# A list scheduler's margins for TensorE behind landings, and preparation ranked by the step that needs it

## The chip, the cores and the metric

The kernel runs on one core of a Trainium2 chip. The metric is the device time of one execution in microseconds; before the change it is 750.58 us, the median of three runs (747.56 to 751.36).

## The reference

Inputs are q, k, v of 4 batches x 8 heads x 768 positions x 64, a projection 64 x 6, and the weights of a gated network. Cut to what matters:

```
q_bucket = sum(bits(q @ proj) * 2**j);  k_bucket = the same of k
mask     = q_bucket[:, :, :, None] == k_bucket[:, :, None, :]
scores   = where(mask, q @ k.T / 8, -1e9)
attn     = softmax(scores);  x = (attn @ v), heads side by side: 4 x 768 x 512
h  = relu(x @ w_in)                       # 512 -> 1024
u, w = h[..., :512], h[..., 512:]
w_n = (w - mean) / sqrt(var + 1e-6)
w_s = einsum('ts,bsd->btd', w_spatial, w_n) + b_spatial[None, :, None]
out = (u * w_s) @ w_out                   # 512 -> 512
```

## The kernel before, in words

**Attention.** The 32 heads are taken as 16 pairs p; head n = 2p + e. A pair has 6 steps i, one for each 128 rows, so there are 96 steps g = 6p + i, written p_i below. A step makes, for both heads, 128 x 768 scores (`scores`, 16 matmuls of 384 columns, tiles `sp`): three products of split float16 halves (`hl`) and a last one of the hash bits (`hk`), which puts masked scores far down. Then for each head VectorE finds the row's bound and copies the scores out (`ex`, L480), ScalarE takes the exponential (`ex`, L483) and its float16 half (`pp`, L487), VectorE or GpSimd ("VG") the rest (`pp`, L491), and a transposing DMA from SyncE's queue turns both (`pt`, L495). TensorE multiplies the turned tiles by v (`weighted`, 18 matmuls, `pv`, L601) some steps later. Heads 2, 4 and 6 work by keys, without turning, and need row maxima first (`row_max`, `mx`).

**Preparation of a pair.** Its q and k are loaded (`load_qk`, 768 KB, one buffer `qk`), hashed (`hash_rows`: 4 matmuls `hp`, two VectorE operations `sg`, 8 small DMAs into `hk`, from GpSimd's queue except for pair 0), and split (`split_qk`: one ScalarE and two VectorE operations, `hl`); v is loaded and split (`load_v`, `split_v`).

**The network.** When 4 pairs (a batch) are done, that batch's network is cut into units of TensorE work (`group`: pieces of 3 matmuls; `vps`, `ups`, `sps`, `ops` by stage), which fill TensorE between the attention steps of the next batch. The last batch's network runs after the last step.

**Weights.** `weights` makes 36 jobs: a load from SyncE's queue (`raw`, four buffers in turn), for 24 of them five more operations (one on ScalarE, four on VectorE, `w`) that make float32 of float64, then two on ScalarE and one on GpSimd that split into halves.

**The planner.** Nothing of this order is written by hand. Every operation is an `Op` with engine, planned duration, predecessors and buffers; `timetable` is a list scheduler: it takes the engine that can start first and, of the operations ready within 0.2 us, the one with the lowest key. The key is `rank` when that is a pair (step, minor), and otherwise (current step, rank), the current step being that of the last planned scores; rank over 8 (the network's units) adds 4 steps. A DMA adds its time to one modelled queue, and its successors get ready when it lands. The operations are then issued in the order of planned starts, so the plan sets only the order of each engine's instructions; on the chip each engine runs them strictly in that order and waits where an operand is not there.

Of the kernel before, what the change touches and what calls it, by code (L numbers as in the profile page):

```python
# [8 lines left out]
F16 = mybir.dt.float16  # L9
# [5 lines left out]
ALU = mybir.AluOpType  # L15
# [3 lines left out]
P = 128  # L19
# [16 lines left out]
def lsh_attention_spatial_gating(  # L36
# [14 lines left out]
    NT = S // P  # L51
    HS = S // 2
# [64 lines left out]
    def timetable(free, banks):  # L117
# [24 lines left out]
        while open_:  # L142
# [95 lines left out]
    def weights():  # L238
# [3 lines left out]
        TINY = 2.0 ** -15 * 1.125  # L242
        RB = 4
        raws = buf("u", UB).new()
# [9 lines left out]
        for i, (src, dst, m, f, key) in enumerate(jobs):  # L254
            c = {}

            def fetch(src=src, m=m, i=i, c=c):
                if i % RB < 2:
                    t = wk.tile([P, NF, HS], F16, tag=f"g{i % RB}", name=f"raw{i}").rearrange("p a q -> p (a q)")
                else:  # L260
                    if i == 2:
                        st["raws"] = wk.tile([P, 2, S], F32, tag="u", bufs=UB, name="raws")
                    t = st["raws"][:, i % RB - 2].bitcast(F16)
# [4 lines left out]
            raw = buf(f"raw{i % RB}", 1).new()  # L268
            hold_ = [raw] if i % RB < 2 else [raw, raws]
            t = op("S", 0.6, fetch, on=hold_, dma=0.95 if src.dtype != F32 else 0.75, rank=R_W)  # L270
# [46 lines left out]
    def load_v(p, *after):  # L317
# [10 lines left out]
        at["v", p] = op("S", 0.5, go, *after, on=[h], rank=R_QK, dma=1.45)  # L328

    def hash_rows(p, *after):  # L330
        qk, k = held["qk", p], (buf("hk", 2) if p != 1 else buf("hk1", 1)).new()
        held["hk", p] = k
        g0, g1 = buf("sg0", 1).new(), buf("sg1", 2).new()
        hp, sg = [], []

        def go():
            hp.append(bank_m(f"hp{p}"))
            for j in range(4):
                nc.tensor.matmul(
                    hp[0][32 * j:32 * j + 32, :HS], lhsT=pj,  # L340
                    rhs=st["qk", p][:, 1 - j // 2, (j % 2) * HS:(j % 2 + 1) * HS],
                    start=True, stop=True, tile_position=(0, 32 * j))

        def bits():
            sg.append(wk.tile([P, HS], F16, tag="sg0", name=f"sg0_{p}"))
            nc.vector.tensor_scalar(sg[0], hp[0][:, :HS], 0.0, hv[:, 0:1], op0=ALU.is_gt, op1=ALU.subtract)

        def scale():
            sg.append(wk.tile([P, HS], F16, tag="sg1", bufs=2, name=f"sg1_{p}"))
            nc.vector.tensor_scalar(sg[1], sg[0], hv[:, 1:2], None, op0=ALU.mult)  # L350
# [3 lines left out]
        t = op("V", 0.3, scale, t, on=[g0, g1], rank=2)  # L354
        at["hk", p] = []
        for j in range(4):
            for e in range(2):
                q, eng = HQ_FIRST[e] if p == 0 else HQ_REST

                def move(j=j, e=e, eng=eng):  # L360
                    eng.dma_start(  # L361
                        out=hkt(p)[D * e:D * e + 2 * NB, 1 - j // 2, (j % 2) * HS:(j % 2 + 1) * HS],
                        in_=sg[1][32 * j + 16 * e:32 * j + 16 * e + 2 * NB, :])
                at["hk", p].append(op(q, 0.53 if q == "G" else 0.75, move, t, on=[g1, k], rank=3, land=2.8 if q == "G" else 1.8))

    def split_qk(p, *after):
# [11 lines left out]
        at["hl", p] = [t] + [  # L378
            op("V", 0.9, lambda to=to, part=part, frm=frm: nc.vector.scalar_tensor_tensor(  # L379
                out=st["hl", p][:, to], in0=st["qk", p][:, part], scalar=SQ, in1=st["hl", p][:, frm],  # L380
                op0=ALU.mult, op1=ALU.subtract), t, on=[qk, h], rank=4)
            for to, part, frm in ((0, 1, 2), (3, 0, 1))]

    def split_v(p, *after):
# [15 lines left out]

        t = op("A", 0.15 + 0.6 * z, high, at["v", p], *after, on=[held["v", p], h], rank=4)
        at["vp", p] = op("V", 0.1 + 0.8 * z, low, t, on=[held["v", p], h], rank=4)

# [65 lines left out]
    def by_queries(p, i, e, g, t, sc):  # L469
# [30 lines left out]
        t = op("A", 0.77, half, t, on=[hx, hp], rank=(g, 1 + e))  # L500
        t = t3 = op("VG", (0.97, 1.68), rest, t, on=[hx, hp], rank=(g, 1 + e))
        at["pt", n, i] = op("S", 1.48, turn, t, on=[hp, ht], rank=(g, 1 + e), dma=TURN)

    def by_keys(p, i, e, g, t, sc):
# [22 lines left out]
        if not wide_:  # L527
            t = op("A", 0.75, half, t, on=[hx, ht], rank=(g, 1 + e))
            t = t3 = op("VG", (0.97, 1.68), rest, t, on=[hx, ht], rank=(g, 1 + e))
        at["pt", n, i] = t  # L530
# [530 lines left out]
```

## Time and the profile before

| | |
|---|---|
| median of the runs | 750.58 us |
| profiled execution, its own time | 750.24 us |
| its span, first to last instruction | 748.4 us |
| TensorE (PE) busy | 631.0 us, 84% |
| VectorE (DVE) busy | 558.5 us, 75% |
| ScalarE (ACT), GpSimd (POOL) busy | 463.5 us, 419.0 us |
| mean granted TensorE clock | 0.945 |
| turning of one `pt`, from issue to landing | 4.1 us, median of 174 |

The times of a profile come from the one profiled execution. PE is a matmul, PEld a weight load. A wait is the idle time of an engine just before an instruction, named by what ended it.

### The profile page before, as it was taken

Reading aid. Unit: us, or ns where it says so; the run is one execution under the profiler, and the core shown is the slowest. Engines: PE = TensorE matmul, PEld = TensorE weight load, DVE = VectorE, ACT = ScalarE, POOL = GpSimd, SP = SyncE. Lnnn points to the kernel's source line nnn. Section 1 sums busy time; section 2 is a strip of 40 time slices with the busy share of each in tenths; the row PEclk is TensorE's granted clock in tenths of the full one; section 3 lists DMA queues with packets and bytes.
Section 4 is the critical chain, followed back from the end, with each engine's and each line's share of the span. In section 5 each row is a group of like instructions: output and inputs, shape, how many; then the busy total and the mean of one; then the engine's idle time right before and its main releaser. Section 6 shows DMA issues by size and latency. Waiting matters only on the chain.

```text
span 748.4 us, 16873 instructions
## 1 busy us (share of the span) xinstructions
PE 631.0 (84%) x6667; PEld 370.7 (50%) x6667; DVE 558.5 (75%) x1009; ACT 463.5 (62%) x707; POOL 419.0 (56%) x451
## 2 busy tenths in 40 slices
PE   3877988967887678789898888879889979989997
PEld 1444755744454445445544545545545445445553
DVE  6889789896999987676879897877677785081250
ACT  3767667787878566656577677566767674332212
POOL 5655554788677669573857565774776552033100
PEclk9788799889998899899999999989999999999999
DMA  5898595799997699899779999897969866001102
GB/s 177 149 201 180 120 218 114 154 223 197 218 222 148 124 188 180 150 187 185 164 166 173 195 149 172 176 174 165 208 122 168 151 117 117 1 1 43 43 1 84
DMA packets 318259, 110.84 MB, mean 148 GB/s; under 512 B 305124, under 2 KB 308196, under 8 KB 318180
## 3 DMA queue, kind: packets, MB, share of 16 engines
q1 hardware_dynamic: 314244, 108.62, 73.9%
q0 software_dynamic: 3840, 1.12, 0.8%
q8 instruction: 52, 0.85, 0.5%
q14 instruction: 27, 0.22, 0.1%
q10 hardware_dynamic: 96, 0.04, 0.0%
HBM read 27.94 MB, written 6.29 MB: 46 GB/s over the span
## 4 chain that ended last, share of the span: by engine, by line
PE 27%; DVE 21%; DMA 13%; issue 10%; ACT 6%; POOL 6%; DVEq 0%; SPq 0%; ACTq 0%; POOLq 0%
DMA pt<-pp 12%; PE sps L696 6%; DVE ex L480 6%; PE ops L696 6%; PE sp L453 4%; DVE pp L491 4%; PE pv L601 4%; ACT pp L487 3%; ACT ex L483 2%; PE ups L696 2%; POOL pp L491 2%; DVE hl L379 2%; PE vpp L696 2%; DVE vr L828 1%; PE vps L696 1%
## 5 line engine op out<-in xcount | busy, mean ns | idle before, releaser
L483 ACT ACTIVATE ex<-ex,nb 128x768 f32<-128x768 f32 x174 | 158.0, 934 | 120.8 <-DVE ex L480 120.5
L601 PE MATMUL pv<-vp,pt 128*128 128x65 f16 (+1 forms) x3132 | 128.3, 198 | 63.7 <-DMA pt<-pp 49.5
L480 DVE TENSOR_SCALAR_CACHE_REDUCE ex<-sp 128x768 f32<-128x768 f32 x174 | 160.0, 949 | 24.9 <-PE sp L453 24.8
L491 POOL TENSOR_TENSOR pp<-ex,pp 128x768 f16<-128x768 f32 x71 | 125.2, 1765 | 88.6 <-ACT pp L487 82.2
L491 DVE TENSOR_TENSOR pp<-ex,pp 128x768 f16<-128x768 f32 x103 | 126.4, 1231 | 57.7 <-ACT pp L487 56.7
L601 PEld LDWEIGHTS <-pt 128*128 128x128 f16 x3132 | 113.7, 100 | 110.3 <-DMA pt<-pp 68.2
L487 ACT CAST pp<-ex 128x768 f16<-128x768 f32 x174 | 138.4, 822 | 0.6
L453 PE MATMUL sp<-hl 64*128 64x384 f16 x1080 | 118.7, 345 | 16.9 <-DVE ex L480 15.6
L696 PE MATMUL sps<-ws,vn 128*128 128x384 f16 x576 | 100.6, 328 | 0.0
L453 PEld LDWEIGHTS <-hl 64*128 64x128 f16 x1104 | 54.0, 98 | 72.3 <-issue 46.1
L361 POOL DMA_DIRECT2D hk<-sg x112 | 59.5, 537 | 43.1 <-PE ups L696 16.0
L696 PEld LDWEIGHTS <-vn 128*128 128x128 f16 x576 | 54.7, 98 | 34.6 <-issue 0.8
L696 PE MATMUL ops<-wo,g 128*128 128x512 f16 x288 | 67.1, 386 | 1.9 <-DVE u L859 1.9
L696 PE MATMUL ups<-xt,wi 128*128 128x384 f16 x348 | 64.2, 333 | 4.3 <-ACT u L864 3.0
L696 PE MATMUL vps<-wi,xt 128*128 128x512 f16 x234 | 56.9, 382 | 2.7 <-ACT vr L779 2.7
L897 POOL TENSOR_TENSOR sy<-sy,u 128x384 f32<-128x384 f32 x24 | 29.3, 1219 | 49.4 <-DVE sy L885 46.4
L633 POOL TENSOR_TENSOR x<-x,xf 128x384 f32<-128x384 f32 x31 | 39.3, 1267 | 26.7 <-DVE x L630 25.9
L453 PE MATMUL sp<-hk 63*128 63x384 f16 (+1 forms) x360 | 51.5, 345 | 2.7 <-DMA hk<-sg 2.7
L696 PEld LDWEIGHTS <-wi 128*128 128x128 f16 x384 | 36.3, 99 | 29.0 <-issue 8.4
L885 DVE SCALAR_TENSOR_TENSOR sy<-sps,bt 128x384 f32<-128x384 f32 x32 | 17.7, 554 | 40.2 <-PE sps L696 40.2
L696 PEld LDWEIGHTS <-g 128*128 128x128 f16 x288 | 27.5, 99 | 33.8 <-issue 4.6
L893 ACT CAST g<-sy 128x384 f16<-128x384 f32 x32 | 16.3, 510 | 42.7 <-POOL sy L897 22.2
(111 smaller groups left out, 855.0 us busy)
## 6 DMA issues: line engine op xcount, KB each, us to landing
qk<-kq SPq DMA_DIRECT2D x16, 768.0 KB, 5.8
out<-o SPq DMA_DIRECT2D x24, 256.0 KB, 4.2
v<-v SPq DMA_DIRECT2D x13, 384.0 KB, 4.7
pt<-pp SPq DMA_TRANSPOSE x174, 4.1
raw<-w_in SPq DMA_DIRECT2D x8, 256.0 KB, 3.5
raws<-w_in SPq DMA_DIRECT2D x8, 256.0 KB
hk<-sg POOLq DMA_DIRECT2D x112, 9.0 KB, 3.5
vf<-v SPq DMA_DIRECT2D x3, 384.0 KB
```

The lines of the kernel that those rows point to most:

```text
L361: eng.dma_start(out=hkt(p)[D * e:D * e + 2 * NB, 1 - j // 2, (j % 2) * HS:(j % 2 + 1) * HS], in_=sg[1][32 * j + 16 * e:32 * j + 16 * e + 2 ...
L453: nc.tensor.matmul(ps[e][:, c - halves[0]], lhsT=src[r, l, rows], rhs=src[r, m, cs], start=(a == 0), stop=(a == len(passes) - 1))
L480: nc.vector.tensor_scalar(ex, st["sc", p, i][e], -ISQ, None, op0=ALU.mult, op1=ALU.min, accum_out=st["nb", n][:, i:i + 1])
L483: nc.scalar.activation(st["e32", n, i], st["e32", n, i], AF.Exp, bias=st["nb", n][:, i:i + 1], scale=-1.0)
L487: nc.scalar.copy(st["pp", n, i][:, 0], st["e32", n, i])
L491: eng.tensor_tensor(out=st["pp", n, i][:, 1], in0=st.pop(("e32", n, i)), in1=st["pp", n, i][:, 0], op=ALU.subtract)
L601: nc.tensor.matmul(o, lhsT=l, rhs=m, start=(i == 0 and k == 0), stop=(i == NT - 1 and k == len(todo_) - 1))
L633: eng.tensor_add(st["x", n], st["x", n], st["f"])
L696: nc.tensor.matmul(c[0], lhsT=l(), rhs=r(), start=(j == 0), stop=(j == len(products) - 1))
L885: nc.vector.scalar_tensor_tensor(out=y[0], in0=c[0], scalar=1.0 / (SN * SW), in1=bt[:, hs], op0=ALU.mult, op1=ALU.add)
L893: nc.scalar.copy(gt[h][0][:, d], y[0])
L897: t1 = op(*POST[last], lambda: either(t1).tensor_mul(y[0], y[0], u[h][:, d]), t, done["u", d, h], on=[hy, hu[h]], rank=2)
```

## The change

Four things are altered, all of them in what the planner is told; the arithmetic stays, and each engine has the same work apart from 5 of the 174 `pp` rests, which move from VectorE to GpSimd.

- When an operation ends, those of its successors that run on TensorE and are not scores are taken as ready later than before: 0.5 us (`LATE`) after an operation of another engine, 2.5 us (`LATE_D`) after a DMA.
- Preparation has a step of its own as rank: hashing and splitting of pair p stand at step 6p - 3 (6p - 8 for pairs with a head by keys), splitting of v at 6p - 1. Before, they counted as of the current step.
- The `pp` rest has planned durations of 1.1 us on VectorE and 1.75 us on GpSimd, before 0.97 and 1.68.
- The weights' loads may be planned 10 us earlier (`W_FROM` 20, before 30). `RB` becomes a list, with the same values i % 4.

```diff
             for a in o.then:
-                a.ready = max(a.ready, come + (0.0 if a.e == o.e and not o.land and not o.dma else X))
+                late = (LATE_D if o.dma else LATE) if a.e == "P" and not (isinstance(a.rank, tuple) and a.rank[1] == 0) else 0.0
+                a.ready = max(a.ready, come + (0.0 if a.e == o.e and not o.land and not o.dma else X + late))
...
-        RB = 4
+        RB = [i % 4 if i < MANY else i % 2 for i in range(36)]
...
+    def urgent(p):
+        return NT * p - (8 if keys(p) else 3)
...
-        t = op("P", 0.8, go, at["qk", p], *after, on=[qk], rank=3, need=("m", 1))
-        t = op("V", 0.62, bits, t, on=[g0], rank=2, gives="m")
+        t = op("P", 0.8, go, at["qk", p], *after, on=[qk], rank=(urgent(p), 3), need=("m", 1))
+        t = op("V", 0.62, bits, t, on=[g0], rank=(urgent(p), 2), gives="m")
...
-        t = op("A", 1.42, high, at["qk", p], *after, on=[qk, h], rank=4)
+        t = op("A", 1.42, high, at["qk", p], *after, on=[qk, h], rank=(urgent(p), 4))
...
-        t = op("A", 0.15 + 0.6 * z, high, at["v", p], *after, on=[held["v", p], h], rank=4)
+        t = op("A", 0.15 + 0.6 * z, high, at["v", p], *after, on=[held["v", p], h], rank=(NT * p - 1, 4))
...
-        t = t3 = op("VG", (0.97, 1.68), rest, t, on=[hx, hp], rank=(g, 1 + e))
+        t = t3 = op("VG", (1.1, 1.75), rest, t, on=[hx, hp], rank=(g, 1 + e))
...
+    LATE, LATE_D = 0.5, 2.5
+    MANY = 36
-    W_FROM, W_EVERY = 30.0, 3.6
+    W_FROM, W_EVERY = 20.0, 3.6
```

In the rows below a name ends in the buffer's running number, the lines after the change stand six further down, and only the first row of each run of matmuls is shown. The first place is TensorE between the scores of steps 9_2 and 9_3 (`sp9_2`, `sp9_3`), before:

```order
L453 MATMUL sp9_2_0_5259<-hl9_4508 128x384
...
L601 MATMUL pv18_5285<-vp1_89,pt18_0_5187 128x65
...
L601 MATMUL pv19_5309<-vp1_89,pt19_0_5218 128x65
...
L696 MATMUL sps0_3_1_5328<-ws0_75,vn0_0_3301 128x384
...
L601 MATMUL pv18_5285<-vp1_89,pt18_1_5307 128x65
...
L453 MATMUL sp9_3_0_5381<-hl9_4508 128x384
```

The same place on TensorE after the change, where `vps1_1` is a unit of the next batch's network:

```order
L459 MATMUL sp9_2_0_5283<-hl9_4462 128x384
...
L607 MATMUL pv18_5304<-vp1_89,pt18_0_5192 128x65
...
L702 MATMUL vps1_0_5022<-wi0_101,xt7_4888 128x512
...
L607 MATMUL pv19_5334<-vp1_89,pt19_0_5221 128x65
...
L702 MATMUL vps1_1_5356<-wi0_101,xt4_3127 128x512
...
L459 MATMUL sp9_3_0_5384<-hl9_4462 128x384
...
L607 MATMUL pv18_5304<-vp1_89,pt18_1_5324 128x65
```

The products of `pt18_1` stood ahead of the scores of 9_3 and stand behind them now; 15 matmuls of 384 columns ahead of them have become 15 of 512 columns.

The second place is the first step of pair 6. On SyncE's queue its q and k (`qk6`) stood, before, ahead of the turning of `pt8_2`:

```order
L265 DMA raws_480<-w_sp 128x384 x2
L313 DMA qk6_2331<-kq 128x1536
L647 DMA_TRANSPOSE xt3_2376<-xs3_2260 128x12x128
L495 DMA_TRANSPOSE pt8_2_2407<-pp8_2_2303 128x12x128
L495 DMA_TRANSPOSE pt9_2_2419<-pp9_2_2306 128x12x128
```

After the change the load stands behind the turning of `pt11_2`, two weight loads just ahead of it:

```order
L501 DMA_TRANSPOSE pt10_2_2882<-pp10_2_2835 128x12x128
L501 DMA_TRANSPOSE pt11_2_2901<-pp11_2_2876 128x12x128
L267 DMA raws_238<-w_out 128x256 x2
L315 DMA qk6_2969<-kq 128x1536
L328 DMA v32_6_2974<-v 128x768
```

It has moved back past 14 turnings, those of seven steps, and with it the hashing of pair 6 on TensorE: `hp6` stood right behind the scores of 5_0 and now stands behind those of 5_5, in the last gap ahead of 6_0, after the change so:

```order
L459 MATMUL sp5_5_0_3102<-hl5_2086 128x384
...
L702 MATMUL ups0_0_0_3095<-xt1_1498,wi0_101 128x384
...
L345 MATMUL hp6_3157<-qk6_2969,hc_73 32x384 x4
L437 MATMUL mp6_3168<-vc6_3139,ones_72 128x128
L607 MATMUL pv10_2919<-vp1_89,pt10_3_3020 128x65
...
L702 MATMUL ups0_3_0_3281<-xt0_1013,wi0_101 128x384
...
L607 MATMUL pv11_2979<-vp1_89,pt11_4_3209 128x65
...
L459 MATMUL sp6_0_0_3370<-hl6_3100 128x384
```

Between `hp6` and the scores stand 42 matmuls of the network, four sets of 18 value products and `mp6`.

The third place is VectorE at the start, where `sg` are the hash bits and `hl` the split of q and k of pair 0, before:

```order
L346 TENSOR_SCALAR sg0_0_121<-hp0_114,hc_73 128x384
L350 TENSOR_SCALAR sg1_0_126<-sg0_0_121,hc_73 128x384
L379 SCALAR_TENSOR_TENSOR hl0_119<-qk0_108,hl0_119 128x768 x2
L398 SCALAR_TENSOR_TENSOR vp0_88<-v32_0_110,vp0_88 128x12x64
L346 TENSOR_SCALAR sg0_1_153<-hp1_144,hc_73 128x384
```

The same place after the change:

```order
L385 SCALAR_TENSOR_TENSOR hl0_114<-qk0_108,hl0_114 128x768 x2
L352 TENSOR_SCALAR sg0_0_129<-hp0_121,hc_73 128x384
L356 TENSOR_SCALAR sg1_0_133<-sg0_0_129,hc_73 128x384
L404 SCALAR_TENSOR_TENSOR vp0_88<-v32_0_110,vp0_88 128x12x64
L352 TENSOR_SCALAR sg0_1_152<-hp1_146,hc_73 128x384
```

The two splits have moved ahead of the hash bits, and so ahead of the DMAs that write `hk`.

More of the change, by code (lines that the diff above doesn't have):

```diff
@@ L257, in fetch @@
             def fetch(src=src, m=m, i=i, c=c):
-                if i % RB < 2:
-                    t = wk.tile([P, NF, HS], F16, tag=f"g{i % RB}", name=f"raw{i}").rearrange("p a q -> p (a q)")
+                if RB[i] < 2:
+                    t = wk.tile([P, NF, HS], F16, tag=f"g{RB[i]}", name=f"raw{i}").rearrange("p a q -> p (a q)")
                 else:
@@ L262, in fetch @@
                         st["raws"] = wk.tile([P, 2, S], F32, tag="u", bufs=UB, name="raws")
-                    t = st["raws"][:, i % RB - 2].bitcast(F16)
+                    t = st["raws"][:, RB[i] - 2].bitcast(F16)
                 c["raw"] = t[:, :m * (4 if src.dtype != F32 else 2)].bitcast(src.dtype)
@@ L267, in weights @@
             z = m / 256
-            raw = buf(f"raw{i % RB}", 1).new()
-            hold_ = [raw] if i % RB < 2 else [raw, raws]
+            raw = buf(f"raw{RB[i]}", 1).new()
+            hold_ = [raw] if RB[i] < 2 else [raw, raws]
             t = op("S", 0.6, fetch, on=hold_, dma=0.95 if src.dtype != F32 else 0.75, rank=R_W)
@@ L363, in move @@
                         in_=sg[1][32 * j + 16 * e:32 * j + 16 * e + 2 * NB, :])
-                at["hk", p].append(op(q, 0.53 if q == "G" else 0.75, move, t, on=[g1, k], rank=3, land=2.8 if q == "G" else 1.8))
+                at["hk", p].append(op(q, 0.53 if q == "G" else 0.75, move, t, on=[g1, k], rank=(urgent(p), 3), land=2.8 if q == "G" else 1.8))
     def split_qk(p, *after):
@@ L380, in split_qk @@
                 out=st["hl", p][:, to], in0=st["qk", p][:, part], scalar=SQ, in1=st["hl", p][:, frm],
-                op0=ALU.mult, op1=ALU.subtract), t, on=[qk, h], rank=4)
+                op0=ALU.mult, op1=ALU.subtract), t, on=[qk, h], rank=(urgent(p), 4))
             for to, part, frm in ((0, 1, 2), (3, 0, 1))]
@@ L399, in low @@
                                            in1=part(x)[:, :, :, D:2 * D], op0=ALU.mult, op1=ALU.subtract)
[L401 to L402 removed]
+        t = op("A", 0.15 + 0.6 * z, high, at["v", p], *after, on=[held["v", p], h], rank=(NT * p - 1, 4))
+        at["vp", p] = op("V", 0.1 + 0.8 * z, low, t, on=[held["v", p], h], rank=(NT * p - 1, 4))
     def mean_v(p, *after):
@@ L528, in by_keys @@
             t = op("A", 0.75, half, t, on=[hx, ht], rank=(g, 1 + e))
-            t = t3 = op("VG", (0.97, 1.68), rest, t, on=[hx, ht], rank=(g, 1 + e))
+            t = t3 = op("VG", (1.1, 1.75), rest, t, on=[hx, ht], rank=(g, 1 + e))
         at["pt", n, i] = t
```

2 lines of the change are left out of this document (1 added, 1 removed).

## The prediction

> **What bounds the kernel now.** I read the page first, for the span and for the chain of work that ended last.
>
> ```profile
> span 748.4 us, 16873 instructions
> PE 631.0 (84%) x6667; PEld 370.7 (50%) x6667; DVE 558.5 (75%) x1009; ACT 463.5 (62%) x707; POOL 419.0 (56%) x451
> ...
> PE 27%; DVE 21%; DMA 13%; issue 10%; ACT 6%; POOL 6%; DVEq 0%; SPq 0%; ACTq 0%; POOLq 0%
> DMA pt<-pp 12%; PE sps L696 6%; DVE ex L480 6%; PE ops L696 6%; PE sp L453 4%; DVE pp L491 4%; PE pv L601 4%; ACT pp L487 3%; ACT ex L483 2%; PE ups L696 2%; POOL pp L491 2%; DVE hl L379 2%; PE vpp L696 2%; DVE vr L828 1%; PE vps L696 1%
> ```
>
> PE is the fullest engine but no engine is full, and the largest single entry of the chain is not computing: it is the turning of `pt`, 12%. An average over stages hides which wait ends last, so the second view is the table by stretches: start, pairs 0 to 3, pairs 4 to 7, pairs 8 to 15, and the end without attention.
>
> ```profile
> core 0: us, PE busy (x) PEld busy (x) DVE busy (x) ACT busy (x) POOL busy (x), PEclk, DMA share, GB/s
> 0.00:12.00 12.00, 3.83 (x20) 1.07 (x22) 8.05 (x12) 3.78 (x4) 6.46 (x17) 1.00 0.50 169
> 12.00:147.00 135.00, 111.49 (x1182) 75.27 (x1179) 117.84 (x235) 91.27 (x144) 79.28 (x94) 0.86 0.79 161
> 147.00:300.00 153.00, 118.33 (x1448) 70.97 (x1449) 135.72 (x239) 115.32 (x183) 114.11 (x115) 0.92 0.96 189
> 300.00:620.00 320.00, 276.89 (x3282) 157.51 (x3281) 250.10 (x436) 213.43 (x304) 198.29 (x204) 0.97 0.89 165
> 620.00:748.40 128.40, 120.44 (x744) 65.85 (x742) 46.77 (x90) 39.69 (x74) 20.91 (x22) 1.00 0.15 41
> ```
>
> Until 300 us DVE is 87 to 89% full (117.84 of 135, 135.72 of 153). From 300 to 620 us it is 78% and PE 87%: PE is idle for 43.1 us there. The third view, PE's waits in that stretch, says for whom:
>
> ```profile
> PE pv L601 <- DMA pt<-pp: 34.3, 29, 2.5
> PE pv L601 <- DVE x L630: 7.5, 4, 2.3
> PE sp L453 <- DVE ex L480: 1.1, 2, 0.5
> ```
>
> These three are the whole 43 us. The scores wait 1.1 us for VectorE, so VectorE does not set the pace in this stretch; PE does, with its stops at value products whose `pt` has not landed. Between 147 and 300 us it is mixed:
>
> ```profile
> PE pv L601 <- DMA pt<-pp: 9.5, 7, 1.9
> PE sp L453 <- DVE ex L480: 9.3, 9, 1.8
> PE pv L601 <- DVE x L630: 6.3, 3, 5.2
> ```
>
> What such a stop does stands in the timeline of PE around step 9_3, the first place of the order:
>
> ```profile
> 362.75 1.15 PE L453 MATMUL sp<-hl 64*128 64x384 f16 x12
> 363.74 0.49 PE L453 MATMUL sp<-hk 63*128 63x384 f16 x4
> 364.23 1.26 PE L601 MATMUL pv<-vp,pt 128*128 128x65 f16 x36
> 365.33 2.60 PE L696 MATMUL sps<-ws,vn 128*128 128x384 f16 x15
> 370.23 0.72 PE L601 MATMUL pv<-vp,pt 128*128 128x65 f16 x18 [2.30 <-DMA pt<-pp]
> 370.88 1.84 PE L453 MATMUL sp<-hl 64*128 64x384 f16 x12
> ```
>
> PE stops for 2.30 us, and the scores of 9_3, which do not need that tile, stand behind the stop; everything that hangs on them starts later.
>
> **The change part by part.** First the margin of 2.5 us. To see what it buys I counted PE's work between a step's scores and its value products in both orders, with durations of this trace:
>
> ```profile
> 344.97 1.41 PE sp L453 x16
> ...
> 347.34 2.92 PE sps L696 x18
> ...
> 352.32 1.20 PE pv L601 x36
> 353.52 1.29 PE vps L696 x6
> ```
>
> At the first place, between `sp9_2` and the products of `pt18_1`, there were 36 value products and 15 matmuls of 384 columns, 1.20 + 15 x 2.92 / 18 = 3.6 us. Now there are 36 value products, 15 matmuls of 512 columns and a set of scores, 1.20 + 15 x 1.29 / 6 + 1.41 = 5.8 us. The difference, 2.2 us, covers the stop of 2.30 us but for 0.1. Over all tiles of pairs 8 to 15 the same count from a tile's own scores to its value products rises from 9.3 to 11.5 us for the first head of a pair and from 11.5 to 13.1 for the second; for pairs 4 to 7 from 9.8 to 11.8 and from 11.7 to 13.6. The stops have a mean of 34.3 / 29 = 1.2 us and a longest of 2.5. So from 300 us on I take four fifths of them away: -27.4 us, with bounds of 0 and -34.3. Between 147 and 300 us VectorE is full and the tiles come later; I take half of 9.5: -4.7, bounds 0 and -9.5.
>
> Second, the clock. Where PE has stood, it runs at half the granted clock next:
>
> ```profile
> 364.00:371.20 7.20, 4.90 (x77) 3.36 (x75) 6.21 (x11) 4.97 (x8) 7.18 (x8) 1.00 0.78 169
> 371.20:374.60 3.40, 3.40 (x36) 1.92 (x31) 2.09 (x5) 1.22 (x3) 3.24 (x4) 0.50 0.79 150
> ```
>
> The same row by row: 1.00 with the stop in it, 0.50 in the 3.4 us behind it. By the table the clock costs (1 - 0.97) x 277 = 8.3 us of PE's time from 300 to 620 us and (1 - 0.92) x 118 = 9.5 from 147 to 300. A third of the 17.8 us goes with the stops: -6, bounds 0 and -14. The Trainium skill speaks against this term: its page TensorE: Matmul & The Clock Gate, in the table of "Why this matters for your kernels", names idle gaps of more than some 3 us as what halves the clock. By that rule stops of at most 2.5 us cost no clock, and the sum would be 6 us higher. The rows do not bear it out: a stop of 2.30 us was enough here, so I keep the term.
>
> Third, the start (third place of the order). The timeline of VectorE before:
>
> ```profile
> 7.43 0.62 DVE L346 TENSOR_SCALAR sg<-hp,hc 128x384 f16<-128x384 f32 x1 [1.37 <-PE hp L339]
> 8.09 0.36 DVE L350 TENSOR_SCALAR sg<-sg,hc 128x384 f16<-128x384 f16 x1
> 8.36 2.07 DVE L379 SCALAR_TENSOR_TENSOR hl<-qk,hl 128x768 f16<-128x768 f32 x2
> ```
>
> The first scores wait for the `hk` landings, which the hash bits set off:
>
> ```profile
> 16.29 0.51 PE L453 MATMUL sp<-hk 63*128 63x384 f16 x2 [2.68 <-DMA hk<-sg]
> ```
>
> With the two splits ahead, the bits end 2.07 us later, less some 0.2 that the splits start earlier: +1.9, between 1 and 3; nothing covers it, since PE has only this to do. The weights' first operations on ScalarE and VectorE, now right ahead and behind of step 0_0's `ex`, lie in waits there. For the rest of the weights' work, the same on each engine and only earlier, I take 0, between -4 and +4: VectorE is 87% full in that stretch whichever way it is dealt.
>
> Fourth, pair 6 (second place). Its load stands seven steps later on SyncE's queue, behind two weight loads that must wait for their buffers, and `hp6` stands in the last gap ahead of 6_0. Durations:
>
> ```profile
> L480 DVE TENSOR_SCALAR_CACHE_REDUCE ex<-sp 128x768 f32<-128x768 f32 x174 | 160.0, 949 | 24.9 <-PE sp L453 24.8
> L483 ACT ACTIVATE ex<-ex,nb 128x768 f32<-128x768 f32 x174 | 158.0, 934 | 120.8 <-DVE ex L480 120.5
> L487 ACT CAST pp<-ex 128x768 f16<-128x768 f32 x174 | 138.4, 822 | 0.6
> L491 POOL TENSOR_TENSOR pp<-ex,pp 128x768 f16<-128x768 f32 x71 | 125.2, 1765 | 88.6 <-ACT pp L487 82.2
> L361 POOL DMA_DIRECT2D hk<-sg x112 | 59.5, 537 | 43.1 <-PE ups L696 16.0
> ...
> qk<-kq SPq DMA_DIRECT2D x16, 768.0 KB, 5.8
> ...
> hk<-sg POOLq DMA_DIRECT2D x112, 9.0 KB, 3.5
> ```
>
> GpSimd takes up the eight `hk` issues behind the `pp` of `pt10_5`, so from the end of the scores of 5_5: two VectorE and one ScalarE exponential step with its half, 2 x 0.95 + 0.93 + 0.82, the rest on GpSimd 1.77, eight issues 8 x 0.54, landing 3.5, together 13.2 us. PE has in that gap 9 + 42 network matmuls (51 x 0.162 = 8.3), four sets of 18 value products (2.4), the hash and a small product (about 1.3): 12.0 us. The scores would stop for 1.2 us, and longer if the load (5.8 us) holds VectorE at `hl6`. I take +3, between 0 and 10. Much work in the gap is drawn from later gaps, not lost.
>
> Fifth, what is late next. With some 30 us less in the way from 300 us on, the same VectorE work falls into less time, 250.1 us in some 290 instead of 320, 86%, near the fill of the stretch before. There the scores waited 9.3 us in 153, which would be 19 in 320; now it is 1.1. I take +8 in between, bounds 0 and 20. The 5 rests that move to GpSimd (1.77 against some 1.23 us each) change little of this, 0. The waits for `x`, 13.8 us, stay: `pv` has two banks and the distance from a pair's last products to the next pair's first stays at about 4 us of PE work in the order.
>
> Sixth, the end: the second unit of `sps2` now stands ahead of the last value products and fills part of the 8 idle us behind 620: -1, between -4 and 0.
>
> Sum: -27.4 - 4.7 - 6 + 1.9 + 0 + 3 + 8 - 1 = -26.2 us. The span of 748.4 becomes 722.2; the profiled execution took 750.24, 1.8 more than its span, so 724.0. The median of the runs lies 0.3 above the profiled one; I say 724.
>
> **The rivals.** *VectorE takes over.* Until 300 us it is 87 to 89% full and the scores wait for it; if the queues behind it behave so at 86% too, 20 us are given back instead of 8, the half of the stops before 300 us is nothing, and the clock gives 3 instead of 6: -26.2 + 12 + 4.7 + 3 = -6.5, 744. For it speaks the first half of the kernel; against it that 250.1 us at 89% would fit into 281 us, so VectorE alone allows 39 us less. The Trainium skill's page Perfetto Trace Analysis, Identifying the Most-Contended Engine, leans to it: matmul busy time is said to be no measure of how near TensorE is to its limit, and occupancy is for the others; by that the 87% of PE count for little and VectorE's 78% for more. The rows agree only until 300 us.
>
> *Preparation comes too late, and the time rises.* If PE does not set the pace from 300 us on, but the chain of scores, `ex`, `pp` and turning does (73% of the chain is not PE), the stops only move, and the hole at pair 6 stays: the load late by its 5.8 us and the split and hash behind it hold the scores of 6_0 by 10 us, and the start costs 1.9: 750.2 + 12 = 762. It decides as soon as the hole costs more than the stops give. Against it: 1.1 us of waiting for `ex`, and in all other pairs from 1 on 16 us of PE work or more still stand between hash and first scores.
>
> *More than I say.* All stops go (-43.8), the clock gives 12, nothing is late next and pair 6 fits: -43.8 - 12 + 1.9 - 1 = -55, 695. Against it: never so far was PE more than 94% full, and 277 of 320 us would become all but full.
>
> That nothing moves is excluded by the order.
>
> **How the numbers follow.** My forecast, with its own range of 710 to 738 us, has 0.56; VectorE taking over 0.18, half of it on each side of the line below; too late 0.15; more than I say 0.11. A measurement can tell about 0.5% of 750.6 us, so faster means under 746.8 and slower over 754.3. Faster: 0.56 + 0.09 + 0.11 = 0.76; the same 0.09; slower 0.15. For 8 in 10 I leave out most of the slower rival (0.13) and the far part of the faster one (0.07): 704 to 750 us.
>
> **What would show it.** Right: PE's waits for `pt` from 300 us to the last scores fall to under 10 us, with the scores of a step ahead of the late products; the granted clock rises over 0.945; scores wait for `ex` between 5 and 12 us there; the last scores end some 25 us sooner; the first scores' `hk` part starts near 18.2 us; a stop of 1 to 10 us at 6_0. Wrong: the stops stay, or turn one for one into waits for `ex`, `x` or `hk`; VectorE stands at `hl6` for over 10 us; the stretch behind the last scores grows.

## The result, and the profile after

The median of four runs after the change is 719.4 us (717.81 to 722.25), of four runs of the kernel before 749.57 us (747.56 to 751.36). The ratio is 0.960, 95% interval 0.956 to 0.9645. Ratios, here and below, leave out single runs that the record marks as slow (one of margin_pv and a few of the kernel before); medians are of all runs. The profiled execution took 722.25 us, its span 720.5, against 750.24 and 748.4 before. The forecast was 724.0.

The head of the page, and the chain of work that ended last:

```profile
span 720.5 us, 16877 instructions
PE 632.9 (88%) x6667; PEld 371.5 (52%) x6667; DVE 550.1 (76%) x1004; ACT 463.1 (64%) x707; POOL 427.0 (59%) x456
...
PE 35%; DVE 28%; DMA 13%; ACT 11%; issue 9%; POOL 2%; SPq 0%; DVEq 0%; ACTq 0%; POOLq 0%
DMA pt<-pp 10%; DVE ex L486 9%; PE sps L702 8%; PE sp L459 7%; PE ops L702 6%; PE pv L607 6%; DVE pp L497 5%; ACT pp L493 4%; ACT ex L489 3%; DVE hl L385 3%; PE ups L702 3%; PE vpp L702 2%; PE mx L459 2%; DVE vr L834 1%; DVE bs L791 1%
```

PE does the same work in nearly the same busy time (632.9 us, before 631.0). Span less busy time is its idle time: 748.4 - 631.0 = 117.4 us before, 720.5 - 632.9 = 87.6 after. So the change took 29.8 us of idle time from PE and added 1.9 us of busy time, 27.9 together. In the chain PE and VectorE have come forward (27 to 35%, 21 to 28%).

The stretches of the prediction were cut at round times. To set like against like they are cut here at the first scores of pair 4, the first scores of pair 8 and the last scores of each kernel; first before, then after (the columns are the prediction's):

```profile
12.00:146.90 134.90, 111.39 (x1181) 75.19 (x1177) 117.74 (x235) 91.17 (x144) 79.28 (x94) 0.86 0.79 161
146.90:310.60 163.70, 126.52 (x1540) 76.15 (x1539) 140.67 (x247) 120.85 (x191) 118.03 (x120) 0.92 0.96 188
310.60:620.00 309.40, 268.80 (x3194) 152.42 (x3192) 245.25 (x429) 208.00 (x296) 194.36 (x198) 0.97 0.89 165
620.00:748.40 128.40, 120.44 (x744) 65.85 (x742) 46.77 (x90) 39.69 (x74) 20.91 (x22) 1.00 0.15 41
```

```profile
12.00:149.10 137.10, 116.94 (x1197) 76.55 (x1195) 112.61 (x235) 95.27 (x154) 81.25 (x94) 0.85 0.79 164
149.10:301.10 152.00, 123.15 (x1493) 73.08 (x1492) 137.57 (x243) 115.42 (x179) 113.36 (x119) 0.93 1.00 188
301.10:598.40 297.30, 275.05 (x3243) 157.74 (x3242) 245.54 (x426) 210.96 (x302) 204.38 (x206) 0.96 0.95 176
598.40:720.50 122.10, 114.57 (x728) 63.20 (x726) 45.75 (x90) 37.92 (x71) 21.11 (x23) 1.00 0.17 43
```

In pairs 8 to 15 PE's idle time falls from 309.4 - 268.8 = 40.6 to 297.3 - 275.05 = 22.2 us. The stretch is 12.1 us shorter only, because 6.3 us more of PE's work stand in it; the stretch behind the last scores has 5.9 us less work and is 6.3 us shorter. In pairs 4 to 7 idle time falls from 37.2 to 28.8, in pairs 0 to 3 from 23.5 to 20.2. VectorE's share in pairs 8 to 15 rises from 79 to 83%.

PE's waits from the first scores of pair 8 to the last scores (total, times, longest), before and after:

```profile
PE pv L601 <- DMA pt<-pp: 31.8, 28, 2.3
PE pv L601 <- DVE x L630: 7.5, 4, 2.3
PE sp L453 <- DVE ex L480: 1.1, 2, 0.5
```

```profile
PE pv L607 <- DVE x L636: 6.5, 3, 5.4
PE pv L607 <- DMA pt<-pp: 5.0, 9, 1.0
PE sp L459 <- DVE ex L486: 4.7, 7, 2.4
PE sps L702 <- ACT vr L785: 2.0, 1, 2.0
PE mp L437 <- POOL xf L625: 2.0, 1, 2.0
```

The stops for `pt` are all but gone. Of the 26.8 us, 3.6 came back as waits of the scores for `ex`, and some 5.5 as single waits that were not there before, the last two rows and three shorter ones. The place of the prediction's first order rows, step 9_2 to 9_3, in PE's timeline after the change:

```profile
351.58 1.15 PE L459 MATMUL sp<-hl 64*128 64x384 f16 x12
352.57 0.49 PE L459 MATMUL sp<-hk 63*128 63x384 f16 x4
352.99 0.72 PE L607 MATMUL pv<-vp,pt 128*128 128x65 f16 x18
353.55 0.81 PE L702 MATMUL vps<-wi,xt 128*128 128x512 f16 x3
354.19 0.71 PE L607 MATMUL pv<-vp,pt 128*128 128x65 f16 x18
354.74 2.75 PE L702 MATMUL vps<-wi,xt 128*128 128x512 f16 x12
357.43 1.15 PE L459 MATMUL sp<-hl 64*128 64x384 f16 x12
358.41 0.49 PE L459 MATMUL sp<-hk 63*128 63x384 f16 x4
358.94 0.72 PE L607 MATMUL pv<-vp,pt 128*128 128x65 f16 x18
```

No row ends in a wait. The products that stopped PE for 2.30 us now stand behind the scores of 9_3, and their tile is there.

### The profile page after: what moved, and what is told of

Its sections match the earlier page's. It is cut to its first block, busy times and chain, and to the rows that moved or that the text cites. A ratio compares the mean times of both kernels' runs of the same rounds, so it can differ in the third digit from the quotient of the medians.

```text
span 720.5 us, 16877 instructions
## 1 busy us (share of the span) xinstructions
PE 632.9 (88%) x6667; PEld 371.5 (52%) x6667; DVE 550.1 (76%) x1004; ACT 463.1 (64%) x707; POOL 427.0 (59%) x456
## 4 chain that ended last, share of the span: by engine, by line
PE 35%; DVE 28%; DMA 13%; ACT 11%; issue 9%; POOL 2%; SPq 0%; DVEq 0%; ACTq 0%; POOLq 0%
DMA pt<-pp 10%; DVE ex L486 9%; PE sps L702 8%; PE sp L459 7%; PE ops L702 6%; PE pv L607 6%; DVE pp L497 5%; ACT pp L493 4%; ACT ex L489 3%; DVE hl L385 3%; PE ups L702 3%; PE vpp L702 2%; PE mx L459 2%; DVE vr L834 1%; DVE bs L791 1%
## 5 line engine op out<-in xcount | busy, mean ns | idle before, releaser
L497 POOL TENSOR_TENSOR pp<-ex,pp 128x768 f16<-128x768 f32 x76 | 136.1, 1792 | 93.2 <-ACT pp L493 85.5
L486 DVE TENSOR_SCALAR_CACHE_REDUCE ex<-sp 128x768 f32<-128x768 f32 x174 | 160.0, 949 | 22.0 <-PE sp L459 21.9
L497 DVE TENSOR_TENSOR pp<-ex,pp 128x768 f16<-128x768 f32 x98 | 123.8, 1266 | 44.8 <-ACT pp L493 43.3
L607 PEld LDWEIGHTS <-pt 128*128 128x128 f16 x3132 | 116.5, 100 | 61.4 <-issue 34.3
L459 PE MATMUL sp<-hl 64*128 64x384 f16 x1080 | 124.5, 351 | 25.4 <-DVE ex L486 23.8
L459 PEld LDWEIGHTS <-hl 64*128 64x128 f16 x1104 | 56.8, 100 | 88.6 <-issue 64.2
L702 PE MATMUL ups<-xt,wi 128*128 128x384 f16 x348 | 66.2, 334 | 2.9 <-DVE sg L352 2.8
L367 POOL DMA_DIRECT2D hk<-sg x112 | 59.5, 537 | 14.7 <-PE pv L607 6.8
L459 PE MATMUL sp<-hk 63*128 63x384 f16 (+1 forms) x360 | 54.7, 348 | 8.4 <-DMA hk<-sg 5.9
L903 POOL TENSOR_TENSOR sy<-sy,u 128x384 f32<-128x384 f32 x24 | 27.2, 1134 | 49.3 <-DVE sy L891 48.9
L891 DVE SCALAR_TENSOR_TENSOR sy<-sps,bt 128x384 f32<-128x384 f32 x32 | 17.7, 552 | 36.2 <-PE sps L702 36.1
L639 POOL TENSOR_TENSOR x<-x,xf 128x384 f32<-128x384 f32 x31 | 34.6, 1115 | 11.1 <-DVE x L636 8.7
L702 PEld LDWEIGHTS <-xt 128*128 128x128 f16 x288 | 25.9, 97 | 29.1 <-issue 3.7
```

The source lines that it names most:

```text
L367: eng.dma_start(out=hkt(p)[D * e:D * e + 2 * NB, 1 - j // 2, (j % 2) * HS:(j % 2 + 1) * HS], in_=sg[1][32 * j + 16 * e:32 * j + 16 * e + 2 ...
L459: nc.tensor.matmul(ps[e][:, c - halves[0]], lhsT=src[r, l, rows], rhs=src[r, m, cs], start=(a == 0), stop=(a == len(passes) - 1))
L486: nc.vector.tensor_scalar(ex, st["sc", p, i][e], -ISQ, None, op0=ALU.mult, op1=ALU.min, accum_out=st["nb", n][:, i:i + 1])
L497: eng.tensor_tensor(out=st["pp", n, i][:, 1], in0=st.pop(("e32", n, i)), in1=st["pp", n, i][:, 0], op=ALU.subtract)
L607: nc.tensor.matmul(o, lhsT=l, rhs=m, start=(i == 0 and k == 0), stop=(i == NT - 1 and k == len(todo_) - 1))
L639: eng.tensor_add(st["x", n], st["x", n], st["f"])
```

## The experiments

The theory: PE runs its instructions strictly in order, so a value product planned for the moment of its tile's landing stops everything behind it whenever the landing is late; the margin puts other work ahead, and that is the gain. Rival one: the other edits (preparation by its step, weights earlier, the durations of the rests) make the gain. Rival two: it is luck, since any edit of the planner deals the order anew. All kernels compute the whole reference. In the table "idle" is PE's (span less busy time of the profiled execution), "8 to 15" the idle time between the first scores of pair 8 and the last scores, "pt" PE's waits for the turned tiles in the whole span, all in us. Busy, idle and pt are of one profiled execution each, which lies between 7.9 us under the kernel's median (late_d1) and 4.9 us over it (after_x016); PE's work is the same in all. The runs were made on several chips, and each ratio is to the kernel before beside it, whose medians were 748.0 to 750.5 us; so differences of medians below are good to some 2 us.

| kernel | median | ratio to before (95%) | PE busy | idle | 8 to 15 | pt |
|---|---|---|---|---|---|---|
| before | 749.57 | 1 | 631.0 | 117.4 | 40.6 | 49.5 |
| after | 719.40 | 0.960 (0.956 to 0.9645) | 632.9 | 87.6 | 22.2 | 5.7 |
| no_margin | 742.89 | 0.991 (0.987 to 0.995) | 635.2 | 110.8 | 41.0 | 54.7 |
| margin_only | 734.05 | 0.977 (0.971 to 0.984) | 634.5 | 96.0 | 25.9 | 8.5 |
| x016 | 739.97 | 0.986 (0.980 to 0.9915) | 627.3 | 109.1 | 32.9 | 56.7 |
| late_d1 | 730.49 | 0.973 (0.967 to 0.979) | 619.7 | 101.2 | 32.1 | 24.5 |
| margin_late | 731.82 | 0.976 (0.9675 to 0.985) | 631.6 | 99.2 | 25.6 | 17.7 |
| margin_pv | 719.11 | 0.958 (0.943 to 0.974) | 623.6 | 93.6 | 21.1 | 10.4 |
| ranks_only | 755.03 | 1.010 (1.006 to 1.013) | 639.3 | 117.0 | 41.3 | 58.2 |
| qk_first | 734.68 | 0.981 (0.9725 to 0.989) | 634.5 | 97.9 | 22.4 | 10.4 |
| pv_only | 729.84 | 0.973 (0.969 to 0.978) | 625.8 | 99.3 | 24.8 | 7.3 |
| after_x016 | 724.76 | 0.9685 (0.9625 to 0.9745) | 633.6 | 94.2 | 27.6 | 10.3 |
| pv_x016 | 724.33 | 0.968 (0.963 to 0.974) | 632.0 | 86.7 | 29.8 | 14.5 |
| landing_only | 733.32 | 0.980 (0.973 to 0.987) | 633.7 | 98.7 | 21.9 | 13.8 |

### The margin alone, everything but the margin, half of it, and an edit that means nothing

**margin_only** is the kernel before with the margins and nothing else of the change:

```diff
+                late = (LATE_D if o.dma else LATE) if a.e == "P" and not (isinstance(a.rank, tuple) and a.rank[1] == 0) else 0.0
-                ... X))
+                ... X + late))
+    LATE, LATE_D = 0.5, 2.5
```

> The kernel before with the margins of 0.5 and 2.5 us alone; ranks, planned durations of the rest and the weights' start are as before. In its order TensorE has 11.4 and 12.9 us of work (first and second head, pairs 8 to 15) between a tile's scores and its value products, as after the change (11.5, 13.1; before 9.3, 11.5). Theory, the margin is the gain: TensorE's stops for pt fall from 49.5 to under 12 us, and the time is 716 to 728 us. Rival, preparation by rank and earlier weights are the gain: 742 to 752 us. Rival, any new plan moves the time by some per cent, whatever it changes: anything from 715 to 760 us, with no tie to the stops.

**no_margin** is the changed kernel with both margins 0:

```diff
-    LATE, LATE_D = 0.5, 2.5
+    LATE, LATE_D = 0.0, 0.0
```

> The kernel after the change with both margins at 0; ranks, planned durations and the weights' start stay changed. TensorE's work between scores and value products is 9.3 and 11.6 us, as before the change. Theory, the margin is the gain: stops for pt 35 to 60 us, time 742 to 755 us. Rival, preparation and weights are the gain: 718 to 728 us. Rival, any new plan moves the time: no tie to the stops.

PE's waits in the whole span, margin_only first (its lines stand one further down than before), then no_margin:

```profile
PE sp L454 <- DVE ex L481: 29.8, 28, 3.9
...
PE pv L602 <- DMA pt<-pp: 8.5, 14, 1.4
```

```profile
PE pv L607 <- DMA pt<-pp: 54.7, 51, 3.5
PE sp L459 <- DVE ex L486: 19.6, 22, 4.8
```

The stops come and go with the margin, whichever of the other edits are there. Taking the margin from the changed kernel costs 742.9 - 719.4 = 23.5 us; giving it to the kernel before brings 749.6 - 734.1 = 15.5 us. So margin_only is 6 us above the expected 716 to 728: its stops are gone and pairs 8 to 15 have 25.9 us of idle time, but its scores wait 29.8 us for `ex`, 26.6 of them ahead of pair 8. (Before, the scores waited 16.1 us for `ex`, after the change 23.8; in the other kernels with a margin it is 25.8 to 40.1 us. So a part of what the margin takes away comes back at VectorE, and how much differs from order to order.)

**x016** changes, in the kernel before, only the planner's price of a handover between engines. It is there to see what dealing the order anew does by itself:

```diff
-    X = 0.15
+    X = 0.16
```

> The kernel before with one neutral number altered: the planner's time from one engine to another is 0.16 instead of 0.15 us, which deals many operations anew. TensorE's work between scores and value products is 9.8 and 12.0 us, half a us above before. Theory: stops for pt 30 to 50 us, time 740 to 752 us. Rival, any new plan moves the time by some per cent: outside 743 to 758 us with stops like before.

The expectation was missed on both counts, the time by a hair and the stops by 6.7 us, and what the rival says came true: the kernel is 1.4% faster with stops no shorter than before (56.7 us against 49.5). So a difference of some 10 us between two orders says nothing of an edit's merit; the margin's 15.5 to 23.5 us are more than that, and its stops tell it apart.

**late_d1** is the changed kernel with half the margin behind a landing:

```diff
-    LATE, LATE_D = 0.5, 2.5
+    LATE, LATE_D = 0.5, 1.25
```

> The kernel after the change with half the margin behind a DMA, 1.25 instead of 2.5 us. TensorE's work between scores and value products is 10.7 and 12.1 us, between before and after. Theory: stops for pt 15 to 25 us, time 726 to 738 us, between the two kernels. Rival, any new plan moves the time: no order with the margin.

The stops lie between (24.5 us), and so does the time. The profiled execution of this kernel was its fastest (722.64 us). Its row for pairs 8 to 15 and its waits there are of use below:

```profile
292.60:586.50 293.90, 261.82 (x3197) 151.10 (x3195) 245.81 (x421) 204.61 (x289) 194.25 (x197) 1.00 0.94 176
```

```profile
PE pv L607 <- DMA pt<-pp: 17.9, 19, 2.9
```

### Which part of the margin, and what the ranks do

**margin_pv** is the changed kernel with the margins for value products alone, none for the network's units and preparation; **pv_only** is the kernel before with these and nothing else of the change:

```diff
-  ... if a.e == "P" and not (isinstance(a.rank, tuple) and a.rank[1] == 0) else 0.0
+  ... if a.e == "P" and isinstance(a.rank, tuple) and 0.5 <= a.rank[1] < 0.7 else 0.0
```

> The kernel after the change with the margins for value products alone; hashes, maxima, network units and means are planned without a margin. Theory: value products carry the gain, so stops for pt stay under 12 us and pairs 8 to 15 take 288 to 299 us; without a margin on hashes and maxima, pairs 0 to 3 take 136 to 145 us; time 708 to 722 us. Rival, the margin works through the network units (their turned operands): stops for pt under 12 us but pairs 8 to 15 at 303 us or more, time 725 to 742 us.

> The order before, with the margins for value products alone (nothing of the ranks, weights or durations). Theory: the margin ahead of value products is the whole gain of pairs 8 to 15. Then pairs 8 to 15 take 286 to 298 us, waits for the turned tiles 7 to 18 us in all, and the time is 718 to 738 us, the rest being what this re-plan makes of the start and the end. Rival: the margin needs the other edits (ranks, earlier weights) to give the after's time; then pairs 8 to 15 take over 300 us or the time is over 740.

Both came out as the theory has it, but for pairs 8 to 15 of margin_pv, which took 287.0 us, 1 us under the range: margins on value products alone give 719.1 and 729.8 us, where margins on all gave 719.4 and 734.1. So the value products carry the margin's gain, as far as these runs can tell. The row of margin_pv for pairs 8 to 15, and the wait of its scores there:

```profile
300.40:587.40 287.00, 265.87 (x3210) 155.21 (x3207) 252.56 (x433) 205.21 (x293) 189.91 (x193) 0.99 0.94 179
```

```profile
PE sp L459 <- DVE ex L486: 8.4, 13, 2.5
```

It has 21.1 us of idle time, as after the change (22.2), with VectorE at 88%, and its scores wait 8.4 us. So from pair 8 on VectorE at this fill does not take over from PE.

**margin_late** gives the changed kernel's margins only from step 24 (pair 4) on, since no_margin is shorter in pairs 0 to 3:

```diff
-  ... if a.e == "P" and not (...) else 0.0
+  ... if step[0] >= 4 * NT and a.e == "P" and not (...) else 0.0
```

> The kernel after the change with the margins applied only from the first step of pair 4 on. So far, pairs 8 to 15 took 297 and 290 us in the profiles with the full margin and 309, 306 and 315 without; pairs 0 to 3 took 162 us with the margin alone, 149 with all changes and 138 with all but the margin. Theory, now in two parts: the margin gains 15 to 20 us from pair 8 on by TensorE's stops for pt, and costs some 10 us in pairs 0 to 3, where it delays hashes and maxima that VectorE's full queue needs. Then pairs 0 to 3 take 135 to 142 us, pairs 8 to 15 288 to 298, and the time is 705 to 716 us. Rival, the length of pairs 0 to 3 is chance of the order: no tie to the margin there, time 715 to 735 us.

Pairs 0 to 3 and 8 to 15 took 139 and 292 us as expected, and still the time is 731.8 us, 16 over the expected 705 to 716 and inside the rival's 715 to 735. Pairs 4 to 7 (158 us, after the change 152) and the stretch behind the last scores (142 us, after the change 122) took it back. In that last stretch stand 132.0 us of PE's work, after the change 114.6: the same network work only moved across the boundary, and what counts is PE's idle time as a whole, 99.2 us against 87.6.

**ranks_only** is the kernel before with preparation ranked by its step, as in the change's diff, and nothing else:

```diff
-        t = op("P", 0.8, go, at["qk", p], *after, on=[qk], rank=3, need=("m", 1))
+        t = op("P", 0.8, go, at["qk", p], *after, on=[qk], rank=(urgent(p), 3), need=("m", 1))
...
```

> The kernel before with preparation ranked by step, and nothing else: no margins, planned durations of the rest and the weights' start as before. TensorE's work between scores and value products is 9.6 and 11.5 us, as before. Theory: stops for pt 40 to 60 us, pairs 8 to 15 306 to 316 us, time 740 to 755 us. If it is the ranks, not the earlier weights, that shorten pairs 0 to 3, these take 136 to 142 us here; if it is the weights, 145 to 152. Rival, preparation by rank is a gain by itself: 718 to 738 us.

It is 1% slower, its idle time in all (117.0) that of before, and its pairs 8 to 15 took 319.6 us, 3.6 over the expected range. The ranks by themselves are no gain. Nor do they shorten pairs 0 to 3: the scores of pair 4 begin at 152.9 us, before at 146.9. In no_margin they begin at 138.0, which must come of its other edits or of the new deal.

**qk_first** is the changed kernel with the loads of q and k ahead of weight loads, to close the hole at pair 6:

```diff
-    R_QK = 0.95
+    R_QK = 0.85
```

> The kernel after the change with the loads of q, k and v ranked ahead of the weights' loads (0.85 instead of 0.95). It undoes the late load of pair 6, whose hash had moved into the last gap and whose first scores came at 237.6 us instead of 225.0. Theory: the hole was filled with network work that is missing nowhere later, so the time stays within 712 to 726 us. Rival, the hole costs what it looks like, 10 us and more: under 711 us. Third, the weights come later for it and the network starts late: over 728 us.

The hole is gone (pairs 6 and 7 start at 219 and 260 us instead of 238 and 268), and the time is 734.7 us, 9 over the expected range and in that of the third case. Its reason shows in part: the network's `sps` units begin at 306.9 us, after the change at 257.3, and 133.4 us of PE's work stand behind the last scores instead of 114.6. PE did network work in the hole, so taking it away won nothing. What the hole itself costs or saves is not shown, since the whole order was dealt anew with it.

### How far a new deal of the order goes

**after_x016** and **pv_x016** are the changed kernel and margin_pv with the edit of x016; **landing_only** is the changed kernel with the margin behind landings alone:

```diff
-    LATE, LATE_D = 0.5, 2.5
+    LATE, LATE_D = 0.0, 2.5
```

> The changed kernel with the planner's price of a step from one engine to another 0.16 instead of 0.15 us, an edit that means nothing in itself. Theory: the gain is the margin's and any re-plan of the changed kernel has it, give or take the 1.4% that the same edit made before: 709 to 730 us, pairs 8 to 15 in 285 to 299 us, waits for the turned tiles 5 to 18 us. Rival: 719 is a lucky draw among orders that differ by more than the margin gives; then over 733.

> Margins for value products alone, with the other edits of the change and the same neutral 0.16 instead of 0.15 us. Theory as for the one before: 709 to 730 us, pairs 8 to 15 in 285 to 299 us. Rival, a lucky draw: over 733.

> The changed kernel with the 0.5 us behind other engines set to 0 and the 2.5 us behind a landing kept. Theory: the landing's margin is the one that matters, so waits for the turned tiles stay under 18 us, pairs 8 to 15 take 286 to 299 us, the time is 712 to 732 us. Rival: the 0.5 us behind other engines (ahead of units of the network and products that wait for ScalarE or VectorE) carries a part; then PE's waits for ScalarE and VectorE other than for ex rise by over 8 us and the time is over 732.

The first two lie 5 us above the kernels they come from: 719 is at the good end of what this change gives, and no draw that stands alone. Pairs 8 to 15 took 297 and 301 us, the second 2 us over the 285 to 299 that were expected. landing_only has its stops down (13.8 us) and missed its upper end by 1.3 us; the waits of PE that the rival names did not rise, so neither case fits. What rose is the scores' wait for `ex`, 37.1 us in all instead of 23.8. That the 0.5 us carries a part of its own is not shown.

All kernels with a margin, the half one too, have 87 to 101 us of idle time and 719 to 735 us; all without have 109 to 117 us and 740 to 755. Rival two could not part them so. It does have a share in the size: the ten times with a margin have their middle at 730 us, the four without at 746, so by a rough estimate from these times some 16 of the 30 us are what a margin is worth apart from the luck of one order. Rival one keeps a remainder: with the margin the other edits together stand for 734.1 - 719.4 = 14.7 and 729.8 - 719.1 = 10.7 us, without it for 749.6 - 742.9 = 6.7. Only the first is clearly more than the 10 us of a new deal, but all have one sign. The ranks alone do not make it; the earlier weights and the new durations were not run alone, so what makes it stays open.

## Why the prediction was right, point by point

**The stops from 300 us on** (-27.4 us): right. Over the same pairs they fell by 31.8 - 5.0 = 26.8 us, and the margin alone does it (margin_only has 6.5 us of them there).

**The stops from 147 to 300 us** (-4.7): under-sized. Between the first scores of pair 4 and those of pair 8 they fell from 12.0 us to 0.6. The step that took half of them because VectorE is full there was wrong in that half; a full VectorE showed as waits for `ex` instead:

```profile
PE sp L459 <- DVE ex L486: 15.8, 20, 2.6
...
PE pv L607 <- DMA pt<-pp: 0.6, 1, 0.6
```

That wait was 9.3 us before, so 6.5 us of the 11.4 came back.

**What is late next** (+8 from 300 us on): the scores' wait for `ex` rose by 3.6 us there, to 4.7 where 5 to 12 had been named, and by 6.5 between pairs 4 and 7. Other waits made up the rest: from pair 8 on all waits but those for `pt` rose from 8.6 to 16.7 us, by 8.1. The size was right, the kind only in part.

**The clock** (-6): this step failed. "A third of the 17.8 us goes with the stops" did not happen: the granted clock was 0.945 before and 0.940 after (0.935 to 0.954 in the four runs). The span stood at half clock for 2 x (1 - 0.945) x 748.4 = 82 us before and for 2 x (1 - 0.940) x 720.5 = 86 us after. By the rows above 38 and 41 us of that lie in pairs 0 to 3, from which the term took nothing. From the first scores of pair 8 to the last there were five spells of 3.4 us at half clock before, each behind a stop for `pt` of 1.75 to 2.33 us. After the change there are four, 20 us together, behind stops for other things. One of the five stops, then the four:

```profile
503.32 0.72 PE L601 MATMUL pv<-vp,pt 128*128 128x65 f16 x18 [1.75 <-DMA pt<-pp]
```

```profile
308.80 0.46 PE L437 MATMUL mp<-vc,ones 128*128 128x128 f32 x2 [2.04 <-POOL xf L625]
...
402.58 0.47 PE L459 MATMUL sp<-hl 64*128 64x384 f16 x1 [2.37 <-DVE ex L486]
...
472.19 1.14 PE L607 MATMUL pv<-vp,pt 128*128 128x65 f16 x18 [5.37 <-DVE x L636]
...
518.11 0.83 PE L702 MATMUL sps<-ws,vn 128*128 128x384 f16 x3 [2.05 <-ACT vr L785]
```

So the stops for `pt` did cost clock, and others, as long or longer, took their place. The table by stretches at the second of the four:

```profile
399.20:402.60 3.40, 1.03 (x22) 0.67 (x19) 3.40 (x5) 1.15 (x3) 3.40 (x3) 0.97 0.31 59
402.60:409.40 6.80, 6.39 (x57) 3.89 (x57) 6.70 (x14) 5.55 (x9) 3.36 (x4) 0.51 0.85 159
```

One stop of 2.37 us for `ex` was followed by 6.8 us at half clock. That a stop need not cost clock shows in late_d1 (its row above): 17.9 us of stops for `pt`, up to 2.9 us each, and a clock of 1.00 throughout, while 1.75 us were enough at 503 us before. So whether a stop costs clock is not read from its kind, its length or the sum of all. The five runs of late_d1, one order, were granted 0.939 to 0.961. The rule of the Trainium skill that the prediction weighed (TensorE: Matmul & The Clock Gate, "Why this matters for your kernels") gave 0 for this term. It came nearer the sum, but not for its reason: 1.75 us before and 2.37 us after, under its some 3 us, were enough here.

**The start** (+1.9, between 1 and 3): right in size. VectorE's row of the first `ex` before, then its rows after:

```profile
16.80 0.96 DVE L480 TENSOR_SCALAR_CACHE_REDUCE ex<-sp 128x768 f32<-128x768 f32 x1 [1.27 <-PE sp L453]
```

```profile
16.74 1.83 DVE L385 SCALAR_TENSOR_TENSOR ws<-qk,ws 128x768 f16<-128x768 f32 x2 [3.12 <-ACT ws L381]
18.48 0.95 DVE L486 TENSOR_SCALAR_CACHE_REDUCE ex<-sp 128x768 f32<-128x768 f32 x1
```

The first `ex` comes 1.7 us later. The way there is longer than was foreseen. The later hash bits hold back the `hk` issues on ScalarE's queue, which end at 15.2 us instead of 12.1. Behind them comes ScalarE's split of pair 1 (buffer `ws`), and VectorE's part of that split stands ahead of `ex`. The last `hk` product started at 18.40 us, where some 18.2 was named.

**Pair 6** (+3): the stop at the scores of 6_0 did not come. PE's timeline after:

```profile
223.60 0.85 PE L345 MATMUL hp<-qk,hc 128*32 128x384 f32 x8 [1.21 <-ACT vr L785]
...
227.38 4.76 PE L702 MATMUL ups<-xt,wi 128*128 128x384 f16 x18 [1.97 <-DVE sg L352]
...
237.62 1.15 PE L459 MATMUL sp<-hl 64*128 64x384 f16 x12
```

Stops of 1.21 and 1.97 us lie ahead of the scores, none at them. They come at 237.62 us, 12.6 later than before, yet pair 8 starts at 301.1 us, before at 310.6. That fits what the prediction says of work drawn from later gaps. qk_first took the hole away and won nothing.

**The end** (-1): the idle time behind the last scores went from 8.0 to 7.5 us. That the stretch is 6.3 us shorter is work done earlier.

The signs that had been named came in part: PE's waits for `pt` from pair 8 on are 5.0 us (under 10 was said) and the last scores end 21.6 us sooner (some 25 was said), but the clock did not rise and no stop stands at 6_0.

Together, over the whole span: the stops for `pt` fell by 49.5 - 5.7 = 43.8 us, PE's idle time by 29.8, so 14.0 us came back as other waits, 7.7 of them for `ex`; PE's busy time rose by 1.9. That is -43.8 + 14.0 + 1.9 = -27.9 us. The prediction had -32.1 for the stops, +11.9 for all that costs idle time (1.9 + 3 + 8 - 1) and -6 for the clock, -26.2. It left out the stops of pairs 0 to 3 (5.3 us) and took 6.7 us too little from pairs 4 to 7. In all the stops fell by 11.7 us more than the sum had, and that made up for the 7.9 us by which the clock failed and the 2.1 more that came back. So the cause and the main term were right, and that the sum lies within 2 us of the result is partly luck. The experiments say so too: without the margin the other edits moved the median by -6.7 us (no_margin), where the sum had +4.9 for them (1.9 + 0 + 3), and an order dealt anew moves by as much.

Of the rivals, *VectorE takes over* did not come from pair 8 on, by the result and by margin_pv; between pairs 4 and 7, where VectorE is 91% full after the change, 6.5 of the 11.4 us did go back to it. *Too late* is refuted by the time itself. *More than I say* was right that nearly all stops go, and failed at the clock and at what is late next.

## What to carry to other kernels

In a static order on an engine that runs in order, an instruction that waits for a transfer belongs well behind the planned landing (here 2.5 us for a turning of 4.1 us), with work that needs nothing of it in between; the stop costs all that stands behind it. One reason for the late landings may be the plan itself: it lets a turning land 0.6 + 1.92 + 0.25 = 2.8 us after its issue when its modelled queue is empty, and the median of all on the chip was 4.1. Whether a longer planned turning would do as well as the margin, or a larger margin better, was not run. Judge such an edit by the wait that it is meant to remove and by the engine's idle time as a whole: lengths of stages only shift work between them, and an edit without meaning moved this kernel by up to 1.4%, so that one new order is no evidence.

## What the runs showed of the hardware

The longest stop after the change behind the first load of q and k, 5.37 us for `x` during pair 12 (its row stands with the clock above), has its cause on VectorE: `x` stands there behind a slow rest. The rests (`pp`) of VectorE from 460 to 476 us (shortest, median and longest in ns), the timeline of VectorE, and that of GpSimd beside it:

```profile
L497 DVE TENSOR_TENSOR pp<-ex,pp x4: 946/1679/4360, 458.6 to 473.3; 128x768 f16<-128x768 f32 x4
```

```profile
464.59 5.23 DVE L497 TENSOR_TENSOR pp<-ex,pp 128x768 f16<-128x768 f32 x2
```

```profile
464.40 1.02 POOL L903 TENSOR_TENSOR sy<-sy,u 128x384 f32<-128x384 f32 x1
465.37 1.78 POOL L906 TENSOR_TENSOR g<-sy,g 128x384 f16<-128x384 f32 x2
467.11 0.99 POOL L639 TENSOR_TENSOR x<-x,xf 128x384 f32<-128x384 f32 x1
468.07 0.97 POOL L624 TENSOR_SCALAR fl<-nb 128x6 f32<-128x6 f32 x1
```

An operation that takes 0.95 us elsewhere took 4.36 us while GpSimd ran four operations of two operands without a gap, and ended within the small one behind them. The Trainium skill's page SBUF — State Buffer (section "Who interferes with whom") says that a VectorE operation with two inputs in SBUF and a GpSimd operation that reads SBUF exclude each other, the later one being blocked until the first ends. The trace agrees in kind; here the block outlasted the first operation and held through three more. In the whole trace after the change, the 20 of VectorE's 98 rests with no GpSimd operation on tensors beside them took 0.944 to 0.959 us, the 29 beside such operations from first to last 1.72 us on average. So the company of GpSimd goes with the slow rests throughout; that the lock is the cause was argued from rows standing side by side, and no run took GpSimd's work away.
